# Earlier turns, deeper gathers and a rearranged end in a fused attention and feed-forward kernel

## The chip, the cores and the metric

The kernel runs on one core of a Trainium2 chip. Times are device microseconds (us) of that core; lower is better. A run over 1.5% above the fastest of its kernel counts as slow and is left out of the ratios. A result is called the same when it lies within 2%. The kernel before takes 592.34 us (median of three runs, 591.86 to 592.80).

## The reference, cut to what matters

Talking-heads attention (the heads are mixed by a 12x12 matrix before and after the softmax) over 8 batches, 12 heads, 448 positions and 64 channels, then a feed-forward network (FFN) of 768 to 2048 to 768 with a squared ReLU.

```python
scores = scale * np.matmul(q, k.transpose(0, 1, 3, 2))
scores = np.einsum('bhij,hg->bgij', scores, w_pre)
attn = softmax(scores)                                   # max, exp, sum (cut)
attn = np.einsum('bhij,hg->bgij', attn, w_post)
x = np.matmul(attn, v)                                   # then (batch, position) rows of 768
h = np.maximum(x @ w_in, 0.0)
return h * h @ w_out
```

## The kernel before

The order of TensorE's (PE's) and GpSimd's (POOL's) instructions is written out by hand; the other engines are VectorE (DVE), ScalarE (ACT) and SyncE (SP, which issues DMAs). The main loop runs over 180 pairs of tiles; a tile is 10 query positions of a batch with all 12 heads in the partitions, 45 tiles a batch. In each pair PE does, in this order: `unmix` of the pair two back, perhaps a turn or some scores, `mix` of this pair, and some units of FFN work for an earlier batch as filler. (`mix` is the mixing of heads before the softmax, `unmix` the one after it; a value unit multiplies its result with v.)

A **turn** transposes a third of a batch's q and k (4 heads), so that scores of the next batch can be computed:

```python
def turn_unit(b, u, copies):
    ...
    for y in range(2):
        for r in range(R):                      # R = 7
            for w in range(2):                  # q or k
                for hh in range(2):             # 2 * 7 * 2 * 2 = 56 transposes of 64x64
                    nc.tensor.transpose(...)
    ...                                         # one copy on DVE, one on ACT

FIRST_TURN = (15, 16, 17)                       # pairs at which batch 1 is turned
TURN = {0: FIRST_TURN, 1: (11, 13, 15), B: (1, 5, 8)}    # later batches: from their start on
```

A **gather** is a DMA from SBUF to SBUF that brings 10 query rows of all heads together in a gather tile. How far gathers run ahead of the mixes is set by the number of these tiles: eight of their own, and six more that live in the last quarter of w2 (`w2_3`) until w2 is loaded there.

```python
AHEAD, LEAD, MORE = 6, 14, 6
HEAD = 2 * (AHEAD + 2 + MORE)                   # up to tile 28 there are 14 gather tiles, then 8
def gather_end(ds):
    return min(2 * ds + AHEAD + 2 + MORE, max(HEAD + AHEAD + 2, 2 * ds + AHEAD + 2))
```

A gather of batch 1 needs the scores of batch 1, and these need its turns. The loads are issued by POOL at given tiles (`at_load(46 + 2 * x, load_v, 1, x)` and so on; two tiles are a pair). At the end, all filler that is left is spent at pair 180, then come the last unmix, the last two value units (`ot_ps`), FFN1 and FFN2 of the last batch:

```python
share = sum(w for w, _ in filler) / rest if now2 else 1e9
...
for j in sorted(timed):
    for _, f in timed[j]:
        f()
fill(1e12)
```

## Time and profile before

The page's busy line, slices and waits stand in the prediction below. This table adds the share of the DMA engines and the clock:

| stretch, us | PE busy us | DMA share | PE's granted clock |
|---|---|---|---|
| 0 to 100 | 69.2 | 0.90 | 0.98 |
| 100 to 200 | 93.5 | 0.72 | 0.97 |
| 200 to 300 | 98.2 | 0.77 | 1.00 |
| 300 to 400 | 99.0 | 0.64 | 1.00 |
| 400 to 500 | 99.5 | 0.68 | 1.00 |

The profile is one execution (span 588.5 us). In rows of PE's timeline, the bracket at the end is the idle time ahead of the group, with what ended it; "issue" means that no wait shows.

### The profile page before, as it was taken

Reading aid. Unit: us, or ns where it says so; the run is one execution under the profiler, and the core shown is the slowest. Engines: PE = TensorE matmul, PEld = TensorE weight load, DVE = VectorE, ACT = ScalarE, POOL = GpSimd, SP = SyncE. Lnnn points to the kernel's source line nnn. Section 1 sums busy time; section 2 is a strip of 40 time slices with the busy share of each in tenths; the row PEclk is TensorE's granted clock in tenths of the full one; section 3 lists DMA queues with packets and bytes.
Section 4 is the critical chain, followed back from the end, with each engine's and each line's share of the span. In section 5 each row is a group of like instructions: output and inputs, shape, how many; then the busy total and the mean of one; then the engine's idle time right before and its main releaser. Section 6 shows DMA issues by size and latency. Waiting matters only on the chain.

```text
span 588.5 us, 28172 instructions
## 1 busy us (share of the span) xinstructions
PE 541.2 (92%) x11810; PEld 306.9 (52%) x11810; DVE 408.1 (69%) x1050; ACT 406.7 (69%) x1223; POOL 399.5 (68%) x599
## 2 busy tenths in 40 slices
PE   3666889899899999999999999999999999999996
PEld 1434656555455555545555556545654555555554
DVE  6666798878687787677777787777777787664011
ACT  3656788668588767886678767886688668861420
POOL 5575678846668955897668865897588667872540
PEclk9999899899899999999999999999999999999999
DMA  9899859967963598448953698459953486433002
GB/s 141 144 219 175 175 101 181 183 117 144 193 141 76 106 188 173 94 86 146 181 132 78 113 192 162 89 88 175 190 108 79 96 146 142 79 68 84 14 25 70
DMA packets 83364, 74.98 MB, mean 127 GB/s; under 512 B 6436, under 2 KB 80164, under 8 KB 83236
## 3 DMA queue, kind: packets, MB, share of 16 engines
q1 hardware_dynamic: 51582, 49.35, 36.0%
q0 software_dynamic: 31264, 23.60, 29.7%
q8 instruction: 92, 1.51, 1.0%
q10 hardware_dynamic: 390, 0.22, 0.2%
q14 instruction: 36, 0.29, 0.1%
HBM read 47.20 MB, written 11.01 MB: 99 GB/s over the span
## 4 chain that ended last, share of the span: by engine, by line
PE 76%; DMA 10%; DVE 3%; ACT 3%; issue 2%; SPq 2%; ACTq 0%; DVEq 0%
PE o_ps L281 25%; PE h_ps L251 24%; PE at_ps L399 9%; DMA G<-S 7%; PE ot_ps L199 6%; PE m_ps L367 6%; PE s_ps L329 4%; DMA w<-S 3%; DVE at L404 2%; PE tr_ps L182 2%; SPq L357 2%; ACT xt L210 1%; ACT e_sb L372 1%; DVE h L260 0%; DVE osb L293 0%
## 5 line engine op out<-in xcount | busy, mean ns | idle before, releaser
L376 POOL TENSOR_SCALAR d<-e_sb,rc 128x448 bf16<-128x448 f32 x360 | 226.5, 639 | 147.8 <-DVE rc L374 146.6
L404 DVE CAST at<-at_ps 128x480 bf16<-128x480 f32 x360 | 219.8, 650 | 66.6 <-PE at_ps L399 57.3
L372 ACT ACTIVATE e_sb<-m_ps 128x448 f32<-128x448 f32 x360 | 195.4, 558 | 26.0 <-PE m_ps L367 21.5
L251 PE MATMUL h_ps<-xt,w 128*128 128x448 bf16 (+2 forms) x960 | 164.2, 319 | 1.4 <-DVE at L404 0.8
L281 PE MATMUL o_ps<-w,h 128*128 128x384 bf16 (+1 forms) x1024 | 163.0, 329 | 0.4 <-issue 0.4
L260 POOL TENSOR_TENSOR h<-hr 128x448 bf16<-128x448 f32 (+2 forms) x136 | 113.8, 846 | 17.1 <-ACT hr L258 17.1
L251 PEld LDWEIGHTS <-w 128*128 128x128 bf16 x960 | 80.3, 99 | 78.1 <-issue 29.0
L281 PEld LDWEIGHTS <-h 128*128 128x128 bf16 (+1 forms) x1024 | 82.8, 101 | 72.3 <-issue 26.9
L333 ACT CAST S<-s_ps 128x448 bf16<-128x448 f32 (+1 forms) x174 | 90.9, 544 | 35.5 <-PE s_ps L329 34.6
L333 DVE CAST S<-s_ps 128x448 bf16<-128x448 f32 (+1 forms) x174 | 104.1, 613 | 0.0
L367 PE MATMUL m_ps<-G,pre 64*64 64x448 bf16 (+2 forms) x696 | 76.4, 357 | 15.5 <-DMA G<-S 10.4
L399 PEld LDWEIGHTS <-d 60*64 60x64 bf16 x5760 | 62.9, 109 | 53.2 <-issue 32.8
L399 PE MATMUL at_ps<-post,d 60*64 60x60 bf16 x5760 | 83.3, 194 | 5.2 <-issue 1.3
L258 ACT ACTIVATE hr<-h_ps 128x448 f32<-128x448 f32 (+2 forms) x160 | 74.1, 487 | 16.7 <-PE h_ps L251 10.7
L374 DVE RECIPROCAL rc<-sm 128x1 f32<-128x1 f32 x360 | 52.7, 157 | 44.2 <-ACT e_sb L372 41.6
L372 ACT ACTIVATION_READ_ACCUMULATOR e_sb<-m_ps 128x1 f32 x360 | 78.7, 219 | 0.0
L210 ACT ACTIVATE xt<-ot_ps,bvec 128x160 bf16<-128x160 f32 (+3 forms) x144 | 44.5, 386 | 48.6 <-PE ot_ps L199 38.8
L329 PE MATMUL s_ps<-kT,qT 64*64 64x448 bf16 x672 | 63.6, 365 | 0.7 <-ACT qT L186 0.3
L288 DVE COPY osb<-o_ps 128x384 f32<-128x384 f32 x48 | 26.0, 547 | 39.5 <-PE o_ps L281 39.3
L367 PEld LDWEIGHTS <-pre 64*64 64x64 bf16 x720 | 28.5, 106 | 37.8 <-issue 31.8
L199 PE MATMUL ot_ps<-at,v 128*64 128x160 bf16 (+4 forms) x1152 | 45.8, 229 | 1.4 <-DVE at L404 1.4
L199 PEld LDWEIGHTS <-v 128*64 128x64 bf16 x1152 | 38.4, 109 | 14.5 <-issue 13.8
(42 smaller groups left out, 210.0 us busy)
## 6 DMA issues: line engine op xcount, KB each, us to landing
G<-S SPq DMA_DIRECT2D x319, 105.0 KB
out_dram<-osb SPq DMA_DIRECT2D x48, 192.0 KB
v<-in_v_dram POOLq DMA_DIRECT2D x32, 192.0 KB, 5.8
qkst<-in_k_dram POOLq DMA_DIRECT2D x24, 224.0 KB, 5.9
qkst<-in_q_dram POOLq DMA_DIRECT2D x24, 224.0 KB, 6.5
w<-in_moe_w_in_dram POOLq DMA_DIRECT2D x8, 384.0 KB, 10.4
w<-in_moe_w_out_dram POOLq DMA_DIRECT2D x8, 384.0 KB, 6.5
out_dram<-osb SPq DMA_DIRECT2D x16, 96.0 KB
```

The costliest lines, as they stand in the source:

```text
L199: nc.tensor.matmul(ps[64 * hh:64 * hh + 64, TW * y + c0:TW * y + 2 + n], lhsT=vs[b][:, g, r, :], rhs=at[:, r, g, c0:2 + n], start=(y == 0 ...
L251: nc.tensor.matmul(ps[:, 0:n], lhsT=w1[ft // 4][:, c2, ft % 4 * 128:ft % 4 * 128 + 128], rhs=xts[b][:, c2, c0:c1], start=(c2 == 0), stop=( ...
L258: nc.scalar.activation(out=hr[:, 0:n], in_=ps[:, 0:n], func=ACT.Relu)
L260: square.tensor_tensor(out=h2ts[(b, ft)][:, c0:c1], in0=hr[:, 0:n], in1=hr[:, 0:n], op=ALU.mult)
L281: nc.tensor.matmul(dst, lhsT=h2ts[(b, ft)][:, mt * 128:mt * 128 + ROWS[mt]], rhs=w2[ft // 4][:, ft % 4, n2 * 384:(n2 + 1) * 384], start=(f ...
L329: nc.tensor.matmul(pss[hh][PR * z:PR * z + PR, 0:S], lhsT=qTs[b][rs, p, PR * j:PR * j + PR], rhs=kTs[b][rs, p, :], start=True, stop=True)
L333: copy(out=Sb[n][z0:z1, 2 * p + hh, :], in_=pss[hh][z0:z1, 0:S])
L367: nc.tensor.matmul(pss[y][64 * x:64 * x + 64, 0:S], lhsT=pre[rows, :], rhs=gs[x][rows, :], start=True, stop=True)
L372: nc.scalar.activation(out=e[:, :], in_=pss[y][:, 0:S], func=ACT.Exp, scale=SCALE, accum_out=sm[:, 0:1])
L376: nc.gpsimd.tensor_scalar(out=d[:, 0:S], in0=e[:, :], scalar1=rc[:, 0:1], scalar2=-1.0 / S, op0=ALU.mult, op1=ALU.add)
L399: nc.tensor.matmul(us[x][PR * z:PR * z + PR, c:c + HR], lhsT=d[rows, j:j + PR], rhs=post[rows, :], start=True, stop=True)
L404: nc.vector.tensor_copy(out=dst, in_=src)
```

## The change

Batch 1 is turned two pairs sooner, batch 2 three. The fourteen gather tiles are kept up to tile 42. Loads of v (batch 1), q and k (batch 2) and w2 come sooner too. At the end, half of the filler is spent at pair 180 and the rest is dealt out between the last value units; the last store's second half goes out on ACT's queue.

```diff
--- before.py
+++ after.py
@@ -32,11 +32,11 @@
 AHEAD = 6
 LEAD = 14
 MORE = 6
-HEAD = 2 * (AHEAD + 2 + MORE)
+HEAD = 3 * (AHEAD + 2 + MORE)
 OFF = 64 - H * (IQ // 2)
 SCALE = 1.0 / 8.0
-FIRST_TURN = (15, 16, 17)
-TURN = {0: FIRST_TURN, 1: (11, 13, 15), B: (1, 5, 8)}
+FIRST_TURN = (13, 14, 15)
+TURN = {0: FIRST_TURN, 1: (8, 10, 12), B: (1, 5, 8)}
 EARLY = [10, 18, 25]
 ROWS = [128, 128, 128, 64]
 
@@ -292,8 +292,8 @@
             osb = ffnp.tile([P, DMODEL], F32, name="osb", tag="osb", bufs=2)
             nc.vector.tensor_copy(out=osb[:, 0:384], in_=ps[:, 0:384])
             r, p = divmod(128 * mt, PR)
-            for n2 in range(2):
-                nc.sync.dma_start(out=out_rows[b, r, p:p + 64, n2 * 384:(n2 + 1) * 384],
+            for n2, eng in enumerate((nc.sync, nc.scalar if b == B - 1 else nc.sync)):
+                eng.dma_start(out=out_rows[b, r, p:p + 64, n2 * 384:(n2 + 1) * 384],
                                   in_=osb[64 * n2:64 * n2 + 64, 0:384])
 
     def ffn1_units(b, c0=0, c1=S):
@@ -447,14 +447,14 @@
             at_load(-1, load_w1, x)
         for x in range(4):
             at_load(-1 if x < 2 else 2, load_v, 0, x)
-            at_load(46 + 2 * x, load_v, 1, x)
+            at_load(44 + 2 * x, load_v, 1, x)
         for x in range(2, 8):
             at_load(1 + x, load_w1, x)
         for x in range(6):
             at_load(11 + 2 * x, load_qk, 1, x)
-            at_load(56 + 2 * x, load_qk, 2, x)
+            at_load(52 + 2 * x, load_qk, 2, x)
         for x in range(8):
-            at_load(24 + 4 * x, load_w2, x)
+            at_load(22 + 3 * x + (4 if x > 5 else 0), load_w2, x)
         for b in range(1, B):
             if b + 2 < B:
                 for x in range(6):
@@ -515,7 +515,7 @@
                 rest = NT // 2
             elif ds <= EARLY[2]:
                 rest = 1 + min(x for x in EARLY if x >= ds) - ds
-            share = sum(w for w, _ in filler) / rest if now2 else 1e9
+            share = sum(w for w, _ in filler) / rest if now2 else sum(w for w, _ in filler) / 2
             now = timed.pop(ds, [])
             for w, f in now:
                 f()
@@ -547,9 +547,14 @@
                 spin(4)
             if ds + 1 < nd + LAG:
                 fill(share)
-        for j in sorted(timed):
-            for _, f in timed[j]:
+        left = [(w, f) for w, f in filler]
+        filler.clear()
+        late = [f for j in sorted(timed) for _, f in timed[j]]
+        for n in range(max(len(late), 3)):
+            for _, f in left[len(left) * n // 3:len(left) * (n + 1) // 3]:
                 f()
+            if n < len(late):
+                late[n]()
         fill(1e12)
 
 
```

## The prediction

> **What bounds the kernel now.** I read the page's busy shares first, then the slices, then PE's own table of waits, then PE's timeline wherever that table has an entry after 50 us. The busy shares and three rows of the slices:
>
> ```profile
> PE   541.2 (92%) x11810; PEld 306.9 (52%) x11810; DVE 408.1 (69%) x1050; ACT 406.7 (69%) x1223; POOL 399.5 (68%) x599
> ...
> PE   3666889899899999999999999999999999999996
> ...
> PEclk9999899899899999999999999999999999999999
> DMA  9899859967963598448953698459953486433002
> ```
>
> PE is the bound: 541.2 of 588.5 us, no other engine above 69%. So the most that any rearrangement can win is PE's 47.3 us of idle time, plus what the clock loses. The row of PE says where that is: before slice 11 (160 us) and in the last slice. The same numbers by stretches of 100 us: busy 69.22, 93.45, 98.20, 99.02, 99.53. So 30.8 us are idle in the first 100 us, 6.6 in the second, then 1.8, 1.0, 0.5. From 160 us on PE is a full queue: whatever is won earlier passes to the end untouched, and what is moved there wins nothing.
>
> PE's waits in the stretch that the change can touch (60 to 170 us) are:
>
> ```profile
> PE m_ps L367 <- DMA G<-S: 4.8, 4, 1.9
> PE tr_ps L182 <- issue: 2.0, 2, 1.8
> PE at_ps L399 <- issue: 1.3, 2, 0.8
> PE m_ps L367 <- DVE at L404: 1.3, 3, 0.5
> PE at_ps L399 <- DVE at L404: 1.0, 1, 1.0
> ```
>
> With three of 0.2 us each they sum to 11.0 us. The largest is a mix waiting for its gather. PE's timeline says which gathers (a mix is four matmuls; the first goes, the other three wait):
>
> ```profile
> 88.06 0.38 PE L367 MATMUL m_ps<-G,pre 64*64 64x448 bf16 x3 [1.86 <-DMA G<-S]
> 92.91 0.38 PE L367 MATMUL m_ps<-G,pre 64*64 64x448 bf16 x3 [0.59 <-DMA G<-S]
> 110.71 0.38 PE L367 MATMUL m_ps<-G,pre 64*64 64x448 bf16 x3 [1.33 <-DMA G<-S]
> 151.15 0.38 PE L367 MATMUL m_ps<-G,pre 64*64 64x448 bf16 x3 [0.98 <-DMA G<-S]
> ```
>
> Counting mixes from the start, these are tile pairs 22, 24, 30 and 45. Pair 22 holds tiles 44 and 45, and 45 is the first tile of batch 1. That is the place the change aims at.
>
> At the other end, the chain that ended last:
>
> ```profile
> 544.11 1.22 DVE at L404 x2
> 545.33 0.04 issue
> 545.37 1.63 PE ot_ps L199 x48
> 547.00 18.45 PE h_ps L251 x96
> 565.45 18.34 PE o_ps L281 x128
> ```
>
> The last value units wait for two casts of DVE while PE has nothing left: PE's timeline puts 1.41 us there. All 14 remaining FFN2 units (72 matmuls, 9.35 us) had been spent before.
>
> **What the Trainium skill says.** "TensorE: Matmul & The Clock Gate", Part 1: too little activity in a free-running window of about 3.4 us halves PE's clock, and a busy window restores it. The trace agrees: the clock is 0.85, 0.83 and 0.83 in the stretches 60 to 70, 110 to 120 and 150 to 160 us and 1.00 beside them; 0.17 of 10 us is 1.7 us, that is 3.4 us at half speed. Each of the three falls on a gap (0.81 us ending at 66.82, 1.33 at 110.71, 1.82 at 154.83). So a gap removed can be worth its length and up to 1.7 us more.
>
> "DMA: Bandwidth & Descriptors", section "Issuing engines are not separate DMA queues": issuing from a second engine saves only the sequencer's time, since the same 16 engines move the data. The trace has that time: the last two stores are issued by SP from 584.40 us, 1.11 us for both.
>
> "Runtime: NRT & Kernel Launch", "Instruction fetch mechanics": instructions are streamed in blocks of 16 KiB by DMA. The trace shows 92 packets, 1.51 MB, in the queue "instruction"; I take the waits marked "issue" at turns (1.82 at 154.83) for a late block, but no row proves it.
>
> **The change part by part.** I walked the schedule of both versions by hand, pair by pair (what is scored, gathered, turned and loaded in each).
>
> (a) *Deeper gathers.* Before, the lead of gathers over mixes is 14 tiles up to pair 11, then no gather is issued in pairs 12 to 14 and the lead falls to 8. After, it stays at 14 through pair 15; gathers stop only at tile 45, which needs batch 1's scores. No instruction is added. The six extra tiles live in the last quarter of w2 until pair 20; its load is at pair 22, so it waits for nothing. Worth by itself: nothing. PE has no gather wait between 60 and 85 us, so the lead there is already enough.
>
> (b) *Turns of batch 1 at pairs 13 to 15 instead of 15 to 17.* The cost is the same: per turn 56 transposes (0.70 us) and two copies (0.91 on ACT, 0.61 on DVE). They press on ACT and DVE: around the old turns PE waited 1.03 for DVE, 0.81 + 0.21 on issue and 0.17. I expect the same 2 us two pairs earlier. The effect is on scores: batch 1's first six pairs of heads (24 to 29) end at pair 18 instead of 20. Tile 45 is gathered at pair 18 instead of 20, with 46 to 49 behind it; four pairs before its mix instead of two. A pair takes about 2.5 us here. The chain of waits says that the late gathers landed after 5.98 and 5.04 us, which two pairs can't cover and four can. So the waits of 1.86 and 0.59 go: **-2.4 us**.
>
> (c) *Loads sooner.* Same bytes (w2 384 KB each, v 192, q and k 224). In pairs 22 to 31 the loads sum to 2,816 KB before and 2,880 KB after; from tile 50 on the lead is 8 tiles in both. So the state that gave 1.33 us at pair 30 (landing 9.14 us after issue, DMA share 1.00) stays; the wait may move or grow. Two w2 loads enter pairs 11 and 12, where PE already waits for gathers (2.6 us at 52 to 58 us). I charge **+0.5 us**.
>
> (d) *Turns of batch 2 at pairs 30, 32, 34 instead of 33, 35, 37.* The scores then run one pair of heads a step instead of alternating 0 and 2. The waits of 0.38 + 0.38 us at pairs 36 and 38 (mix behind a cast) and 0.53 on issue at pair 34 sit right beside the old turns. The new ones stand in a denser stretch of FFN1. I take half: **-0.6 us**. Tile 83, the first to need batch 2, is gathered in pair 38 in both versions.
>
> (e) *The last FFN2 units.* Seven stay in pair 180; seven are dealt out 2, 2, 3 around the last two value units. The first two are 8 matmuls of some 0.16 us, 1.3 us under the casts of 1.22. The wait of 1.41 falls to about 0.1: **-1.3 us**. The shorter run ahead of the last unmix is harmless: 28 matmuls are 4.6 us, and its inputs were mixed at 532.1 us.
>
> (f) *The last store's second half on ACT's queue.* One issue is 1.11 / 2 = 0.55 us. If the two queues overlap fully the end comes that much sooner, if they share the generator not at all: **-0.3 us**.
>
> (g) *The clock.* Three halvings cost 3 x 1.7 = 5.1 us. The first moves with the turns, the other two stand on the gaps at pairs 30 and 46, which I expect to stay. A chance of about 0.3 to lose one of them: **-0.5 us**.
>
> Sum: -2.4 + 0.5 - 0.6 - 1.3 - 0.3 - 0.5 = -4.6 us, so 592.34 - 4.6 = **587.7 us**, 0.8% faster.
>
> **Rivals.** *1. The wait only moves on.* Gathers that no longer wait for scores now queue behind the two w2 loads of pairs 22 and 23, and pairs 25 to 31 wait instead. For it: the DMA share of 1.05 and 1.00 at 90 to 110 us and landings of 9.14 us against a lead of some 10. Against it: no byte is added and the engines were at 0.72 and 0.54 from 70 to 90 us, which the earlier loads fill. Then only the tail is won: about 590.5 us.
>
> *2. The clock decides.* If the activity of a long stretch counts and the change lifts it, both later halvings vanish: 2 x 1.7, and with the waits of pairs 22 and 24 that gives about 584 us. For it: none occurs after 160 us, where PE is 99% busy. Against it: each one coincides with a gap that I expect to stay. A new halving is as possible: 589.5 us.
>
> *3. ACT and DVE become the bound at 58 to 70 us.* DVE is 5.72 and ACT 5.63 of 6 us busy from 60 to 66 us, at only the first of the old turns. Turning at pairs 13 to 15 puts that load directly behind the waits of pairs 11 and 12. It could add 1 us, or take 1 away because PE's waits give the others time to catch up.
>
> **Range and chances.** The tail (1.6 us) is nearly sure. The 2.4 us is likely, with some of it returned under rival 1. Clock and instruction fetch give about 2 us either way, and the three runs of before spread over 0.94 us. That makes 584.2 to 590.6. The 2% mark is 11.8 us, at 580.5: it would take both halvings and nearly every wait of the table. I give it 0.02, and 0.01 to a loss of that size, which only a wait on a load not yet landed at a turn could bring; the last load is issued three pairs (7.5 us) before its turn and lands in about 6.
>
> **What would show it.** (b): no gather wait at pairs 22 and 24; PE's gather waits in 60 to 170 us down from 4.8 to about 2.4. (c): the wait at pair 30, or near it, still there at 1 to 2 us; no wait for w2, v or q, k. (d): the cast waits at pairs 36 and 38 gone. (e): the value units at the end with less than 0.3 us before them. (f): one ACT issue beside the last SP issue. (g): clock dips counted again by stretches. PE's busy time should stay at 541, less 1.7 for each dip lost. The prediction is wrong if the gather waits keep their sum, or if the number of dips changes by two.

## The result

The changed kernel takes **588.37 us** (median of four runs, 586.88 to 589.78) against 592.38 us before. The ratio is 0.9932, with a 95% interval of 0.9906 to 0.9959: about 4 us, or 0.7%, faster, and by the 2% rule the same. A ratio is the mean time of one kernel's fast runs over that of the other's fast runs of the same rounds, so it isn't quite the ratio of the medians that are quoted.

Later runs of both kernels spread far more. The kernel before took 588.5 to 597.6 us in 33 further runs, one of them slow (mean 592.8), the changed one 583.3 to 592.1 in six. So one execution, and thus one profile, says little of a difference of 2 us. Three rows of slices and the busy line of the page of the changed kernel (the fastest of the four runs, span 585.1 us):

```profile
PE   536.6 (92%) x11810; PEld 304.7 (52%) x11810; DVE 407.0 (70%) x1050; ACT 407.3 (70%) x1223; POOL 399.3 (68%) x599
...
PE   2666698889899999999999999999999999999997
...
PEclk9989999999999999999999999999999999999999
DMA  9899979948963698548953698449953486442103
```

PE's busy time fell by 4.6 us although it does the same 11,810 matmuls: the clock was halved once between 20 and 200 us in this execution, against three times in that of before. Two halvings fewer, each 3.41 us at half speed, make 3.4 us of it; the rest isn't traced. PE's table of waits between 60 and 170 us, the largest five:

```profile
PE at_ps L399 <- issue: 4.5, 3, 2.4
PE m_ps L367 <- DMA G<-S: 2.0, 2, 1.8
PE tr_ps L182 <- issue: 1.8, 2, 1.1
PE at_ps L399 <- POOL d L376: 1.7, 6, 0.4
PE tr_ps L182 <- DMA qkst<-in_q_dram: 1.1, 1, 1.1
```

The waits for gathers fell from 4.8 to 2.4 us (with 0.4 that is booked on the `w` tiles, the gather tiles in w2), just as predicted. But all PE waits of this stretch together were not fewer: 13.9 us against 11.0. The rise itself is within the spread of executions: two runs below have 13.6 with the old middle (`tail_only`) and 13.2 with the new one again (`after_again`). PE's timeline of the changed kernel says where the waits were:

```profile
65.17 0.38 PE L367 MATMUL m_ps<-G,pre 64*64 64x448 bf16 x3 [1.75 <-DMA G<-S]
71.40 0.22 PE L399 MATMUL at_ps<-post,d 60*64 60x60 bf16 x4 [2.37 <-issue]
110.40 0.64 PE L182 MATMUL tr_ps<-ident,qkst 64*64 64x64 bf16 x56 [1.13 <-DMA qkst<-in_q_dram]
120.87 0.28 PE L399 MATMUL at_ps<-post,d 60*64 60x60 bf16 x10 [1.52 <-issue]
153.04 0.35 PE L182 MATMUL tr_ps<-ident,qkst 64*64 64x64 bf16 x19 [1.12 <-issue]
```

The waits at pairs 22 and 24 are gone. New are a gather wait at pair 14 (65.17), a wait of the first turn of batch 2 for q (110.40), and larger waits marked "issue" than in the profile of before. The end of the chain of waits:

```profile
537.95 1.41 PE o_ps L281 x8
539.36 0.84 PE ot_ps L199 x24
540.20 1.53 PE o_ps L281 x12
541.72 0.72 PE ot_ps L199 x24
542.44 1.95 PE o_ps L281 x24
544.39 18.27 PE h_ps L251 x96
```

DVE's casts have left the chain; PE passes from one group to the next without a gap. And the last store, first in the timeline of the kernel before, then in that of the changed one:

```profile
584.40 1.11 SPq L296 DMA_DIRECT2D out_dram<-osb  x2
```

```profile
581.61 0.47 SPq L296 DMA_DIRECT2D out_dram<-osb  x1
581.61 0.58 ACTq L296 DMA_DIRECT2D out_dram<-osb  x1
```

Two issues in a row took 1.11 us; side by side they take 0.58. From the last copy's start to the end of the span it was 4.64 us and is now 4.08.

### The profile page after: what moved, and what is told of

It reads as the page before. It is cut to its first block, busy times and chain, and to the rows that moved or that the text cites. A ratio compares the mean times of both kernels' runs of the same rounds, so it can differ in the third digit from the quotient of the medians.

```text
span 585.1 us, 28172 instructions
## 1 busy us (share of the span) xinstructions
PE 536.6 (92%) x11810; PEld 304.7 (52%) x11810; DVE 407.0 (70%) x1050; ACT 407.3 (70%) x1223; POOL 399.3 (68%) x599
## 3 DMA queue, kind: packets, MB, share of 16 engines
q0 software_dynamic: 31264, 23.60, 29.9%
## 4 chain that ended last, share of the span: by engine, by line
PE 74%; DMA 10%; DVE 4%; ACT 3%; issue 2%; SPq 1%; POOL 1%; ACTq 0%; DVEq 0%; POOLq 0%
PE o_ps L281 24%; PE h_ps L251 24%; PE at_ps L399 9%; DMA G<-S 8%; PE ot_ps L199 6%; PE m_ps L367 6%; PE s_ps L329 3%; DVE at L404 2%; PE tr_ps L182 2%; ACT xt L210 2%; DMA w<-S 1%; SPq L357 1%; ACT e_sb L372 1%; DMA out_dram<-osb 1%; POOL d L376 1%
## 5 line engine op out<-in xcount | busy, mean ns | idle before, releaser
L251 PE MATMUL h_ps<-xt,w 128*128 128x448 bf16 (+2 forms) x960 | 162.3, 316 | 2.3 <-DVE at L404 1.6
L251 PEld LDWEIGHTS <-w 128*128 128x128 bf16 x960 | 79.1, 98 | 78.3 <-issue 29.5
L281 PEld LDWEIGHTS <-h 128*128 128x128 bf16 (+1 forms) x1024 | 82.2, 101 | 70.5 <-issue 25.4
L399 PE MATMUL at_ps<-post,d 60*64 60x60 bf16 x5760 | 84.6, 194 | 10.9 <-issue 4.9
L367 PE MATMUL m_ps<-G,pre 64*64 64x448 bf16 (+2 forms) x684 | 73.7, 354 | 11.1 <-DMA G<-S 6.9
L367 PEld LDWEIGHTS <-pre 64*64 64x64 bf16 x720 | 27.8, 106 | 32.2 <-issue 23.8
```

The costliest lines, as they stand in the source:

```text
L251: nc.tensor.matmul(ps[:, 0:n], lhsT=w1[ft // 4][:, c2, ft % 4 * 128:ft % 4 * 128 + 128], rhs=xts[b][:, c2, c0:c1], start=(c2 == 0), stop=( ...
L281: nc.tensor.matmul(dst, lhsT=h2ts[(b, ft)][:, mt * 128:mt * 128 + ROWS[mt]], rhs=w2[ft // 4][:, ft % 4, n2 * 384:(n2 + 1) * 384], start=(f ...
L367: nc.tensor.matmul(pss[y][64 * x:64 * x + 64, 0:S], lhsT=pre[rows, :], rhs=gs[x][rows, :], start=True, stop=True)
L399: nc.tensor.matmul(us[x][PR * z:PR * z + PR, c:c + HR], lhsT=d[rows, j:j + PR], rhs=post[rows, :], start=True, stop=True)
```

## The experiments

My theory after the first comparison: the end wins about 2 us, the earlier turn of batch 1 wins some 2 us more, and part of it is given back at places that the change made: w2's early loads, batch 2's early turn, and "issue". The first rival: the middle nets nothing, and the end is the whole gain. The second: run-to-run noise of the clock is all there is beside the end. Every kernel had one profile and five timed rounds (six runs), and every one gave correct results. Differences in us are differences of the mean times of fast runs to the kernel before on the same chip, with their standard error; the ratios pair runs of the same rounds and differ a little.

### The end alone, the rest alone, and the whole once more

`tail_only` is the kernel before with three edits of the diff: the last store's queue, `share`, and the rearranged end. `middle_only` is the changed kernel with those undone. `after_again` is the changed kernel.

> The kernel before with only the end of the change: half of the last 14 FFN2 units in pair 180, the rest dealt out around the last two value units, and the last store's second half on ACT's queue. My theory (prediction parts e and f, and the two traces, in which the stretch from the last mix to the end of the span is 2.0 us shorter) says 1.6 to 2.0 us faster than before, ratio 0.9966 to 0.9973, with no PE wait ahead of the last value units. Rival: the end is worth all of the measured 4.0 us, ratio about 0.993, if the middle of the change nets nothing. Second rival: the clock and the fetches vary so much from run to run that the gain does not show, ratio 0.999 to 1.000.

> The change without its end: earlier turns of batches 1 and 2, gather tiles up to 42, earlier loads; end as before. If the parts add up and the end is worth 1.6 to 2.0, this is 2.0 to 2.4 us faster than before, ratio 0.9960 to 0.9966, as the prediction had it. Rival: the profile of the changed kernel shows 13.9 us of PE waits between 60 and 170 us where the kernel before has 11.0, so without luck of the clock the middle is worth nothing or costs up to 1 us: ratio 0.999 to 1.002. In both cases the profile should have no gather wait at pairs 22 and 24, and waits on gathers at pairs 13 and 14 and on the q load at the first turn of batch 2.

> The changed kernel once more, on the same chip as the three below, because single runs of every kernel spread over 3 to 9 us. Expected 588 to 590 us and a ratio to before of 0.993 plus or minus 0.004. In its profile the same waits as in the first profile should come back if they are of the kernel and not of chance: a gather wait at pair 14 (1.75 before), a wait ahead of the first turn of batch 2 (1.13), and waits marked issue of which every one stands at the same places of PE's instruction stream (positions 193 modulo 256).

| kernel | median us | ratio | 95% interval | difference, us |
|---|---|---|---|---|
| end alone | 590.15 | 0.9941 | 0.9880 to 1.0002 | -2.9 +- 1.5 |
| rest alone | 589.59 | 0.9950 | 0.9895 to 1.0005 | -3.0 +- 1.3 |
| whole | 588.71 | 0.9943 | 0.9898 to 0.9989 | -3.7 +- 1.3 |

Times alone don't settle the shares: each half seems to win nearly as much as the whole, with a standard error that is about half of it. The traces do better, because most of the noise sits in one place. I took the times at which the last matmul of given mixes starts, and the stretches between them, from the fourteen traces (mix 179 is the last):

| kernel | 12 to 22 | 29 to 39 | 60 to 179 | 179 to end |
|---|---|---|---|---|
| before | 30.3 | 29.9 | 337.7 | 56.33 |
| end alone | 34.9 | 28.6 | 338.7 | 54.30 |
| rest alone | 28.9 | 31.2 | 338.3 | 56.33 |
| whole, first profile | 29.5 | 28.6 | 337.8 | 54.32 |
| whole, second profile | 30.5 | 29.7 | 337.3 | 54.30 |

The last column is 54.29 to 54.32 in all eleven traces with the new end and 56.33 to 56.34 in all three without. **The end is worth 2.03 us**, in every execution. Of it 1.41 is the wait for the casts and 0.56 the last store. From pair 60 to 179 all versions take the same time within 0.8% (337.3 to 340.0 us). Most of the rest, gain and noise, lies in the first 60 pairs: the start of mix 60 scatters with a standard deviation of 2.2 us over the fourteen traces, the stretch after it with 0.7. There the same instructions took 30.3 us in one execution and 34.9 in another (the first two rows are the same program up to mix 179), so what the middle is worth can't be read from two profiles. It even depends on where one starts to count: from the first matmul of mix 12, whose others wait for their gathers, the five rows of 12 to 22 read 30.9, 35.7, 31.4, 32.2 and 32.9.

Of the first rival that leaves this: the whole less the end is 2.0 us in the first comparison and 1.7 +- 1.3 in this one, so that the rest nets nothing is unlikely but not excluded.

The repeat also brought the same new waits: 1.33 us for a gather at pair 14, 2.46 for q ahead of batch 2's first turn, and 1.86, 0.94, 0.66 and 0.94 marked "issue".

### Batch 1's turn, and the gather tiles

`b1_only` is the kernel before with two edits, and nothing else of the change:

```diff
-HEAD = 2 * (AHEAD + 2 + MORE)
-FIRST_TURN = (15, 16, 17)
+HEAD = 3 * (AHEAD + 2 + MORE)
+FIRST_TURN = (13, 14, 15)
```

> The kernel before with parts a and b alone: gather tiles up to 42 and batch 1 turned at pairs 13, 14, 15; loads, batch 2 and end as before. Theory (prediction, parts a and b): the gather waits at pairs 22 and 24 (1.86 and 0.59 us) go; there is no gather wait at pairs 13 and 14, because the w2 loads are not early; no wait for q ahead of batch 2's turns. So 1.5 to 2.5 us faster than before, ratio 0.996 to 0.9975. Rival: the turns move two pairs into a stretch where PE's blocks are already fetched late, and the waits marked issue give it back: ratio 0.999 or more.

Measured: 589.57 us, ratio 0.9945 (0.9892 to 0.9999), -3.1 +- 1.5 us. By the 2% rule that is the same, and the interval only just excludes no change. Its table of PE's waits between 60 and 170 us starts with

```profile
PE at_ps L399 <- issue: 2.5, 1, 2.5
PE m_ps L367 <- DMA G<-S: 1.8, 1, 1.8
```

The one gather wait is at 145.96 us. There is none at pairs 22 and 24, none at 13 and 14, none ahead of a turn: 9.0 us of waits in all against 11.0 before.

`head_old` is the changed kernel with `HEAD = 2 * (AHEAD + 2 + MORE)` again.

> The changed kernel with one edit undone: the fourteen gather tiles used up to tile 28, as in the kernel before, instead of 42. Everything else (turns, loads, end) as changed. My theory (prediction, part a): the deeper lead is worth nothing by itself; time within 1 us of the changed kernel (588 to 589 us), no gather wait between pairs 15 and 21. In detail tile 45 is gathered one pair later, at pair 19, so a small gather wait, at most 0.6 us, may come back at pair 22. Rival: without it the gathers are short in pairs 12 to 21, and 1 us or more of gather waits return there: 590 us or more.

Measured: 586.68 us, ratio 0.9896 (0.9850 to 0.9943), -6.0 +- 1.1 us. No gather wait between 66 and 149 us, so none in pairs 15 to 22. Without the deeper gathers the kernel is no slower than with them (588.4 and 588.7, on other chips), and perhaps faster. Why it should be faster isn't shown; with a standard error of over 1 us for each, it may be chance.

### Where part of it was given back: w2, and batch 2

`w2_late` and `b2_late` each undo one part of the changed kernel:

```diff
-            at_load(22 + 3 * x + (4 if x > 5 else 0), load_w2, x)      # w2_late
+            at_load(24 + 4 * x, load_w2, x)
```

```diff
-TURN = {0: FIRST_TURN, 1: (8, 10, 12), B: (1, 5, 8)}                   # b2_late
+TURN = {0: FIRST_TURN, 1: (11, 13, 15), B: (1, 5, 8)}
-            at_load(52 + 2 * x, load_qk, 2, x)
+            at_load(56 + 2 * x, load_qk, 2, x)
```

> The whole change, but w2 loaded at the tiles of the kernel before (24, 28, ... 52 instead of 22, 25, ... 47). The theory: the new gather waits at pairs 13 and 14 (0.43 and 1.75 us) come from two w2 loads now issued at pairs 11 and 12, so they shrink to under 0.6 us together, and the kernel is 0.5 to 1.6 us faster than the changed one (587.0 to 587.9 against 588.4). Rival: those waits come from the chance order of DMA traffic in the first 50 us and stay; then the time is that of the changed kernel within 0.5 us, or up to 1 us longer because two w2 loads meet the loads of v and q, k at pairs 24 and 26.

> The whole change, but batch 2 turned at pairs 33, 35, 37 and its q, k loaded from tile 56 as in the kernel before. The theory: the earlier turns of batch 2 save the two cast waits of 0.38 us but pay 1.13 us for q that has not landed at pair 30 and 1.5 us at a block border of PE's instruction stream; so undoing them gives a kernel 0.5 to 2 us faster than the changed one, without the wait for q. Rival (my prediction, part d): the early turns win 0.6 us, so undoing them costs 0.6 us.

With w2 late: 591.41 us, ratio 0.9968 (0.9913 to 1.0023). The gather waits of pairs 13 and 14 vanished, as the theory had it; but the time didn't fall to the 587.0 to 587.9 that it expected. In the trace the last w2 load, issued at pair 26, meets the first loads of q and k for the early turn of batch 2, and that turn waits longer than in any other trace. The row from PE's timeline:

```profile
111.88 0.96 PE L182 MATMUL tr_ps<-ident,qkst 64*64 64x64 bf16 x56 [4.47 <-DMA qkst<-in_q_dram]
```

Over all fourteen traces, the gather waits of pairs 13 to 15 are 1.0 to 2.4 us in eight of the nine kernels with early w2 loads (the ninth, `shift128` below, stood 1.3 us at "issue" just before), and nothing in the five without. So the early w2 loads are the cause of these waits. What they cost in time I can't say: in two kernels that differ in nothing else (`spread` and `spread_w2late` below, on two chips) the medians are 585.97 and 585.67.

With batch 2 late: 586.91 us, ratio 0.9908 (0.9851 to 0.9965), -5.5 +- 1.4 us, and no wait for q. The stretch from mix 29 to 39 holds both versions of these turns. It takes 26.2 to 32.2 us in the eight traces with batch 2 early (mean 29.4) and 27.4 to 29.9 in the six with it late (mean 28.2). In seven of the eight the first turn waited 1.1 to 4.5 us; in two of these seven the profile books it on a cast of DVE, at the same instruction. In the six it never waited. So the early turn of batch 2 wins nothing, and seems to **cost** about 1.2 +- 0.75 us.

When that q load landed is told in three of the seven traces: 7.8 us after its issue in the repeat of the changed kernel, 8.1 in `middle_only` (just before the turn, so the wait booked on DVE there was for q too) and 9.7 in `w2_late`. PE stood at the turn 5.3 to 5.4 us after the issue. The load of the repeat, from a view of its DMAs at 103.0 us:

```profile
qkst<-in_q_dram POOLq DMA_DIRECT2D x1, 224.0 KB, 7.8
```

### What "issue" is

In the trace of the changed kernel I numbered PE's instructions from 0 (weight loads, matmuls, and a few others at the start). The five waits marked "issue" come ahead of numbers 2497, 4801, 5057, 6337 and 6849. All of these are 193 modulo 256. Two of the five of the kernel before, as rows:

```profile
66.82 0.37 PE L399 MATMUL at_ps<-post,d 60*64 60x60 bf16 x20 [0.81 <-issue]
...
154.83 0.35 PE L182 MATMUL tr_ps<-ident,qkst 64*64 64x64 bf16 x19 [1.82 <-issue]
```

They are number 2241 and 6337: 193 modulo 256 again. The Trainium skill ("Runtime: NRT & Kernel Launch", "Instruction fetch mechanics") has blocks of 16 KiB, 256 instructions. The queue "instruction" has 92 packets of 16,384 bytes, and PE 23,660 instructions, which is 92.4 blocks. The packets' times, from the trace's DMA records of the changed kernel:

| border at number | border before, us | fetch in the DMA record, us | last instruction ahead of the border | PE goes on |
|---|---|---|---|---|
| 2497 | 66.44 | 69.09 to 70.00 | 68.84 | 71.40 |
| 4801 | 115.72 | 117.76 to 119.26 | 119.16 | 120.87 |
| 5057 | 120.87 | 122.06 to 123.21 | 123.84 | 124.69 |
| 6337 | 147.60 | 150.59 to 151.55 | 151.73 | 153.04 |
| 6849 | 158.14 | 161.63 to 162.62 | 163.15 | 164.00 |

In these five a block's fetch starts 1.2 to 3.5 us after the border before it, and PE goes on 1.4 to 1.6 us after the packet's end. A turn is 56 transposes and 56 weight loads in 0.7 us; an unmix is 64 more instructions. Two turns in neighbouring pairs empty a block in 2.4 us (66.44 to 68.84).

To test this, `shift80` and `shift128` add matmuls of 16 columns, never read, in the opening, where PE waits for the first gather. They move the borders to other instructions of the program.

```diff
+        pad = bank("pad_ps")
+        for _ in range(40):                                            # shift128: 64
+            nc.tensor.matmul(pad[0:64, 0:16], lhsT=ident[0:64, 0:64], rhs=ident[0:64, 0:16], start=True, stop=True)
         spin(4)
```

> The changed kernel with 40 matmuls of 16 columns, never read, in the opening where PE waits 2.4 to 2.7 us for the first gather: 80 more PE instructions, so the borders of the 256-instruction blocks fall 80 instructions earlier in the program. Theory: the waits marked issue are PE waiting for its next block, whose fetch takes about 4.4 us from the border before; any block executed faster stalls. From the trace of the changed kernel I work out 2.6 to 3.1 us of such stalls for this shift against 5.0 us unshifted, and at other places of the program: near 64, 95, 112 and 122 us, not at the old ones (70, 119, 151). So 2 us faster than the changed kernel, 586 to 588 us. Rival: the waits belong to the transposes or to memory traffic at fixed times; then they stay at 70, 119, 124 and 153 us, and the time is that of the changed kernel.

> As the run before, with 64 such matmuls: 128 instructions of shift, half a block. Theory: 6.9 us of stalls, the worst of the shifts that I worked out, with the largest near 153, 163 and 175 us (1.6, 1.7 and 1.0 us) where the changed kernel has 1.12 and 0.66; so 4 us slower than the shift of 80 and 2 us slower than the changed kernel, 590 to 592 us. Rival: as before, no difference from the shift of 80 beyond 1 us.

Rows from PE's timeline, first of the shift of 80, then of 128:

```profile
98.05 1.25 PE L251 MATMUL h_ps<-xt,w 128*128 128x160 bf16 x9 [1.71 <-issue]
...
166.47 0.37 PE L399 MATMUL at_ps<-post,d 60*64 60x60 bf16 x22 [0.83 <-issue]
```

```profile
69.71 0.48 PE L182 MATMUL tr_ps<-ident,qkst 64*64 64x64 bf16 x20 [3.25 <-issue]
...
166.41 0.84 PE L281 MATMUL o_ps<-w,h 128*64 128x384 bf16 x8 [0.98 <-issue]
```

The rule of place held: every wait marked "issue" again stood at 193 modulo 256 of the shifted stream, so at other instructions of the program; the ones near 71, 121 and 153 us were gone with the shift of 80, and 98 us had a new one ahead of an FFN1 matmul, where there is no transpose near. The sizes mostly missed. For 80 the sum came out (2.83 us against 2.6 to 3.1), but of the four places only 64 and 95 (98) did. For 128 I had the largest stalls near 153, 163 and 175 us; they came at 64, 70 and 166. The times were 589.58 us (ratio 0.9960; I had 586 to 588) and 594.16 us (0.9990, with two of six runs slow; I had 590 to 592). The 4.6 us between the medians are the 4 us that I had worked out, but the fast runs alone differ by only 1.8, so in time this is **inconclusive**.

All 14 traces together have 66 waits of PE marked "issue" between 25 and 200 us, of 0.19 to 3.78 us, and every one is at 193 modulo 256. Of the blocks between 40 and 260 us, sorted by how fast PE ran through them; the pause is from the start of the last instruction ahead of the border to the start of the next:

| block run in | blocks | with a pause of over 0.15 us | mean pause, us |
|---|---|---|---|
| under 2.5 us | 7 | 6 | 1.68 |
| 2.5 to 3.5 us | 50 | 30 | 0.66 |
| 3.5 to 4.5 us | 80 | 27 | 0.29 |
| 4.5 to 5.5 us | 145 | 26 | 0.11 |
| over 5.5 us | 261 | 19 | 0.03 |

So "issue" on PE is, in this kernel, the wait for the next block of instructions, and it comes mostly, though not each time, where PE runs through a block in less than about 5 us. When a fetch starts varies: at border 2497 it was from 0.4 us before to 4.2 us after the border before it in the fourteen traces. The 4.6 us between the first two rows of the table of stretches are largely this: at that border PE waited 0.21 us in the one execution and 3.78 in the other.

### Turns spread out

If so, turns want a pair between them. `b1_spread` is the changed kernel with this one edit; `spread` has `b2_late`'s edits as well; `spread_w2late` has those of `w2_late` too.

```diff
-FIRST_TURN = (13, 14, 15)
+FIRST_TURN = (11, 13, 15)
```

> The changed kernel with one edit: batch 1 turned at pairs 11, 13, 15 instead of 13, 14, 15; batch 2 stays early. Theory: a free pair between turns cuts the stall at the block border near 70 us (2.56, 2.05, 0.84 and 2.9 us in the four traces with adjacent turns) to about 1.2, and the first turn partly lies under gather waits: 1 to 2 us faster than the changed kernel, 586.5 to 587.5. The wait for q ahead of batch 2's first turn (1.1 to 4.5 us in the traces with early turns of batch 2) stays. Rival: the gain of the earlier run with both edits came only from batch 2's later turns; then 588 to 589 us.

> The changed kernel with the turns of batch 2 and their loads as in the kernel before (which gave 586.9 to 587.5 us in the first set), and batch 1 turned at pairs 11, 13 and 15 instead of 13, 14 and 15. Theory: a turn is 112 PE instructions in 0.7 us, so two turns in neighbouring pairs empty a block in 2.4 us, against some 4.4 us for the fetch of the next; one pair between them takes the largest stall (2.4 to 2.7 us, at 69 to 71 us) down below 1 us, and the first turn goes under the gather waits of pairs 11 and 12. So 2 us faster than without it: 585 to 586 us. Rival: q, k of batch 1 have not landed at pair 11, and the turn waits for them 1 us or more; then no gain, 587 to 588 us.

> The best version by the runs so far: the changed kernel with batch 2's turns and loads as before, batch 1 turned at pairs 11, 13, 15, and w2 loaded at the tiles of the kernel before. Theory: with w2 late the gather waits of pairs 13 and 14 (0.67 and 0.67 us with the early w2 loads and the same turns) go, as they did in the run with late w2 alone, and no q load is there to collide with: 584.5 to 586 us, ratio 0.987 to 0.990. Rival: the last w2 loads then meet those of v at pairs 24 and 26, and 1 us or more of gather waits appears in pairs 26 to 31: 586.5 to 588 us.

| kernel | median us | ratio | 95% interval | difference, us | mix 12 to 22, us |
|---|---|---|---|---|---|
| whole change (twice) | 588.4, 588.7 | 0.9932, 0.9943 | see above | -3.7 +- 1.3 | 29.5, 30.5 |
| b1_spread | 587.31 | 0.9903 | 0.9850 to 0.9957 | -5.2 +- 1.3 | 27.7 |
| b2_late | 586.91 | 0.9908 | 0.9851 to 0.9965 | -5.5 +- 1.4 | 31.4 |
| spread | 585.97 | 0.9898 | 0.9865 to 0.9931 | -6.3 +- 1.0 | 26.8 |
| spread_w2late | 585.67 | 0.9878 | 0.9835 to 0.9921 | -7.1 +- 0.9 | 25.4 |

The last column flatters the three kernels with spread turns, since one of their three turns lies before mix 12. A fairer measure is when the last matmul of mix 22 starts: at 85.4 to 86.1 us in these three traces, at 85.5 to 90.1 in the nine with turns at pairs 13, 14 and 15 (means 85.9 and 87.5, a difference of 1.6 +- 0.5 us). The wait marked "issue" near 70 us is 0.81 us in `b1_spread`, 1.00 in `spread` and none in `spread_w2late`. Of the nine traces with turns at pairs 13, 14 and 15, seven have 0.41 to 3.25 us there, and two (`b1_only` and the shift of 80) none, so a single wait doesn't prove the point. In times, neither `b1_spread` differs from the whole change nor `spread` from `b2_late` by more than the error, so what spreading alone wins isn't shown. In `spread` the first turn waited 0.31 us for q and then 1.20 at a border, under the gather waits of pairs 11 and 12; the rival was thus right in a small part. The last version is the fastest: 7.1 +- 0.9 us ahead of the kernel before on the same chip (by the 2% rule still the same), some 2.7 ahead of the changed one, which ran on other chips; its six runs spread over only 2.8 us. The top of its table of PE's waits between 60 and 170 us:

```profile
PE h_ps L251 <- DVE at L404: 1.5, 3, 0.7
PE at_ps L399 <- issue: 1.4, 2, 0.7
PE at_ps L399 <- POOL d L376: 1.2, 4, 0.4
PE m_ps L367 <- DMA w<-S: 1.1, 1, 1.1
PE m_ps L367 <- DMA G<-S: 1.0, 3, 0.5
```

No row is over 1.5 us any more; the 1.1 is the tail of a wait at pair 12.

## Why the prediction was right or wrong

The time was right: 587.7 us predicted, 588.37 measured, inside the range. Not every step was.

- **(a) deeper gathers, worth nothing by themselves: right**, as far as the runs resolve. Without them the time is 586.68 us, so they win nothing.
- **(b) batch 1's turn, -2.4 us: right in the mechanism.** The waits at pairs 22 and 24 are gone in every trace with the earlier turn. Alone, with the gather tiles, it is worth -3.1 +- 1.5 us, which agrees with the size but hardly tests it.
- **(c) the loads, +0.5 us: the mechanism was half right, the place wrong.** I had the wait at pair 30 stay. It went, and 1.0 to 2.4 us of gather waits appeared at pairs 13 to 15 instead. I had looked for the collision of the early w2 loads at pairs 11 and 12, where they are issued, but a gather issued then is waited for only some pairs later.
- **(d) batch 2's turn, -0.6 us: wrong.** It costs about 1.2 +- 0.75 us. The step that failed is in my last lines on chances: "the last load is issued three pairs (7.5 us) before its turn and lands in about 6". The 6 us are a median over the whole kernel, and at pairs 26 to 31 the DMA share is 1.0 (100 to 115 us): there q landed after 7.8 to 9.7 us where the trace tells it, and PE was at the turn 5.3 to 5.4 us after the issue. The first turn waited 1.1 to 4.5 us in seven traces of eight. Nor did the cast waits go: in place of twice 0.38 us at pairs 36 and 38, all eight traces have 0.38 at pair 35 and 0.17 to 0.18 and 0.29 to 0.30 us for POOL just after mix 38.
- **(e) and (f), the end, -1.6 us: right, a little too small.** It is 2.03. The wait of 1.41 went entirely. The term that I had mis-sized is the store: 0.56 us in place of 0.3, since the two queues' issues overlap fully. That agrees with what "DMA: Bandwidth & Descriptors", "Issuing engines are not separate DMA queues", says: what is won is about one issue.
- **(g) the clock, -0.5 us: not resolved.** The first profile had two halvings fewer. But the mean granted clock is 0.9855 over 33 runs of the kernel before (0.976 to 0.997) and 0.9872 over ten of the changed one (0.980 to 0.997): a lucky profile, not a mended clock. By my own sign ("if the number of dips changes by two") this profile spoke against the prediction; the repeat has four dips.
- **Fetches**, which I had only in the width of the range: the waits marked "issue" between 60 and 170 us sum to 3.5 and 6.0 us in the two profiles with the old middle (`before`, `tail_only`) and to 6.3, 4.4 and 3.5 in the three with the new one (`after`, `after_again`, `middle_only`). So they vary by more than the change moves them. My guess that they are late blocks was right; what I missed is that moving the turns moves them against the borders.

The sum of the parts, -2.0 (end) - 3.1 (batch 1) + 1.2 (batch 2) = -3.9 us, agrees with the -4.0 and -3.7 measured, with 1.5 us of doubt in the second term and 0.75 in the third. That the forecast of -4.6 came so near is in part luck: too little for the end, and a gain forecast for batch 2 and the clock that didn't come, cancelled in part. Of the rivals, the first ("the wait only moves on") was true for a good part of the middle: the waits between 60 and 170 us were not fewer in the changed kernel (13.9, 13.2 and 11.9 us with the new middle, 11.0 and 13.6 with the old). What stays open: how much time the early w2 loads cost, why the kernel with fewer gather tiles was not slower, and what decides when a block's fetch starts, which makes most of the 4.6 us between two executions of the stretch from mix 12 to 22.

## What to carry to other kernels

Where one engine is full for most of the time, noise and gain sit in the few stretches where it isn't: measure those stretches in several traces, since a single profile can show a lucky clock as a gain. Moving a load sooner pays only if it lands in time at that place, so take its landing time from that stretch and not from a median. And it's worth trying to spread dense bursts of small PE instructions: a block of 256 run in under some 5 us may be waited for at its end (here 6 of 7 under 2.5 us, 26 of 145 between 4.5 and 5.5).

## What the Trainium skill lacked or had wrong

- "Runtime: NRT & Kernel Launch", "Instruction fetch mechanics", calls the cost of crossing a 16 KiB border mostly hidden. Here 66 waits of up to 3.78 us stand at such borders in 14 traces, and blocks run in under 2.5 us had a pause of 1.68 us each on average. It says nothing of the time of a fetch: between border and restart 5.0 us in the median of the 61 gaps of over 0.5 us at borders between 40 and 260 us (3.0 to 6.9), of which 1.4 after the packet's end.
- The same section gives PE room for 2,048 instructions, while its note below says that the memory is only two lines of 16 KiB. The traces fit the note, one block ahead: with the packets counted in order, the fetch for a border starts 0.9 us (median; -3.8 to 4.8) after the border before it over 1,261 blocks of the fourteen traces, and 2.6 us (-0.2 to 4.4) in the 61 gaps.
- "TensorE: Matmul & The Clock Gate", Part 1: the window of 3.41 us is as it says (some halvings last two). But it has the clock halved after an idle window, and here half idle was enough: between 25 and 250 us of the fourteen traces, 41 windows at full clock were followed by a halved one, and PE was busy (by its matmul records) for 20 to 58% of each; of the 806 followed by another at full clock, none was busy for under 50%. It says that the start varies from run to run, but lacks a figure for a whole kernel: here a mean clock of 0.976 to 0.997 in 33 runs of the same program.
- "Perfetto Trace Analysis", "DMA Instruction — HWDGE (DVE, Sync)", has the generator locked for one issuer at a time; here SP's and ACT's issues both start at 581.61 us and take 0.47 and 0.58, so no such wait is seen.
